# Mixture-of-experts stage: fixed blocks of 448 slots per expert with stationary weights, and the general path behind one branch at the end

## Chip, cores, metric

The kernel runs on one core of one Trainium2 chip. The metric is device time in microseconds (us), the median of several runs. The engines are called PE (matmul; PEld is its weight load), DVE, ACT, POOL and SP, as in the profile.

## The reference

A linear attention (RWKV5) over 4 batches x 8 heads x 768 steps x 48 gives 3072 tokens of 384 values. Each token goes to one of 8 experts. The expert is the argmax of 8 logits or, where a gate is open, the expert of the token before:

```python
for b in range(B):
    prev_e = -1
    for s in range(S):
        fresh_e = int(np.argmax(logits[b, s]))
        if s == 0 or local_gate[b, s] < 0.5:
            e = fresh_e
        else:
            e = prev_e if prev_e >= 0 else fresh_e
        prev_e = e
        ...                                   # p = softmax of the logits
        h = np.maximum(x[b, s] @ w1[e], 0.0)  # 384 -> 1024
        out[b, s] = p[e] * (h @ w2[e])        # 1024 -> 384
```

Everything is fp32. With the fixed input the experts get 417, 353, 336, 448, 376, 390, 329 and 423 tokens.

## The kernel before

Four stages follow one another: a chunked attention (with a branch to a general version, for decay weights outside a range); a routing on DVE that gives every token a slot; the experts; the end. Slots are cut into tiles of 128, each tile belonging to one expert. How many tiles an expert needs is only known at run time, so the loop runs over the worst case:

```python
NT = (N + E * (P - 1)) // P          # 31 tiles of 128 slots
...
with tc.If(outside > 0, label="general"):          # between attention and routing
    general_attention(...)
...
def fetch(j):                                       # weights anew for every tile
    e = nc.values_load(tex[0:1, j:j + 1], ...)      # the tile's expert, from memory
    nc.sync.dma_start(out=w1t..., in_=w1[bass.ds(e, 1)]...)
    nc.sync.dma_start(out=w2t..., in_=w2[bass.ds(e, 1)]...)
    nc.gpsimd.indirect_dma_start(out=xg, in_=x_d, in_offset=...gid[:, j:j + 1]...)
def hidden(j):                                      # w1 stationary, 128 tokens moving
    for m ...: for kk ...:
        nc.tensor.matmul(hps[:, m * P:(m + 1) * P], lhsT=w1[:, 4 * g + m, kk, :], rhs=xT[:, kk, :], ...)
def output(j):                                      # hT stationary, 384 columns of w2 moving
    for m in range(FK):
        nc.tensor.matmul(yp[:, :D], lhsT=hT[:, m, :], rhs=w2[:, m, :], ...)
    nc.vector.tensor_scalar(yo, yp[:, :D], gate[:, j:j + 1], None, Alu.mult)
    nc.gpsimd.indirect_dma_start(out=out, out_offset=...sid[:, j:j + 1]..., in_=yo, ...)
```

(`...` marks cuts.)

## Time and profile before

The median is 569.85 us (569.43 to 570.50, 4 runs). The table of windows, cut at the seams of the stages, shows where they go. Its columns are the window, its length, the busy time (and instructions) of PE, PEld, DVE, ACT and POOL, the granted TensorE clock, the DMA share and GB/s.

```profile
0.00:182.60 182.60, 158.47 (x1342) 115.31 (x1342) 134.94 (x326) 16.17 (x33) 93.06 (x61) 1.00 0.59 201
182.60:216.70 34.10, 13.18 (x56) 11.89 (x56) 17.77 (x61) 0.36 (x1) 3.87 (x14) 0.55 0.46 186
216.70:222.71 6.01, 0.87 (x3) 0.50 (x4) 0.56 (x2) 0.00 (x0) 4.03 (x4) 0.50 0.33 88
222.71:560.81 338.10, 338.10 (x2074) 272.03 (x2074) 35.28 (x60) 37.02 (x62) 56.69 (x58) 0.99 0.84 301
560.81:568.70 7.89, 0.00 (x0) 0.00 (x0) 0.62 (x1) 0.00 (x0) 0.98 (x1) 0.74 0.00 0
```

| stage | us | what sets its length |
|---|---|---|
| attention | 182.6 | untouched by the change |
| branch and routing | 34.1 | a serial chain, most of it DVE instructions; 10.5 us of it are matmuls |
| first gather and turn | 6.0 | one gather and its transposes (the turn), then the expert matmuls can begin |
| experts | 338.1 | PE: busy in every microsecond |
| end | 7.9 | scaling, one scatter, closing drain |

In the fourth row PE's busy time equals the length of the window, so the stage can only get shorter if PE gets less to do.

### The profile page before, as it was taken

The page shows a single profiled execution, that of the slowest core. Times are in us where ns is not written, and L with a number is a line of the kernel's source. Part 1 is how long each engine was busy: PE and PEld are TensorE (multiplying, and loading weights), DVE is VectorE, ACT ScalarE, POOL GpSimd, SP SyncE. Part 2 cuts the span into 40 slices and gives each one's busy share as a digit, 9 for nine tenths or more (in the row PEclk, how much of TensorE's full clock was granted, in tenths as well). Part 3 has the DMA queues.
Part 4 walks back from the last instruction along what each step waited for, and adds up shares of the span by engine and source line. Part 5 has one row for each costly group of instructions (what it writes and reads, how often), then busy time and mean ns, then how long its engine had stood idle before and what let it go on. Part 6 is the DMA issues. An engine that isn't in the chain of part 4 may idle for free. (4 is left out here: it accounts for less than half of the span.)

```text
span 568.7 us, 8584 instructions
## 1 busy us (share of the span) xinstructions
PE 510.6 (90%) x3475; PEld 399.7 (70%) x3475; DVE 189.2 (33%) x449; ACT 53.5 (9%) x96; POOL 158.6 (28%) x136
## 2 busy tenths in 40 slices
PE   0689999999998155999999999999999999999994
PEld 0567587577584155878877877887887887887782
DVE  6699679589491650111011011110110101101100
ACT  0000200200202000100110110110110011011010
POOL 6578466277211013122121121221211212110010
PEclk9999999999999555999999999999999999999998
DMA  8678847854202084688899899988899989998830
GB/s 299 225 251 283 299 165 249 278 169 155 95 29 85 2 349 164 241 319 319 320 325 338 301 341 330 327 319 335 312 330 335 321 321 311 330 311 326 306 112 0
DMA packets 28412, 145.41 MB, mean 256 GB/s; under 512 B 4336, under 2 KB 7439, under 8 KB 20432
## 3 DMA queue, kind: packets, MB, share of 16 engines
q1 hardware_dynamic: 20448, 128.98, 64.2%
q0 software_dynamic: 3968, 10.82, 5.2%
q10 hardware_dynamic: 3952, 5.00, 2.5%
q8 instruction: 29, 0.48, 0.3%
q14 instruction: 15, 0.12, 0.1%
HBM read 135.35 MB, written 10.81 MB: 257 GB/s over the span
## 5 line engine op out<-in xcount | busy, mean ns | idle before, releaser
L490 PEld LDWEIGHTS hps<-exT,w1t 128*128 128x128 f32 x1488 | 172.8, 194 | 9.0 <-DVE exT L481 1.1
L490 PE MATMUL hps<-exT,w1t 128*128 128x128 f32 x1488 | 173.1, 277 | 0.7 <-DVE exT L481 0.7
L498 PE MATMUL eyp<-w2t,hT 128*128 128x384 f32 x496 | 165.1, 486 | 0.0
L498 PEld LDWEIGHTS eyp<-w2t,hT 128*128 128x128 f32 x496 | 91.8, 190 | 57.5
L502 POOL DMA_INDIRECT out_dram<-yo,sid x31 | 31.2, 1006 | 174.9 <-DVE yo L501 174.9
L481 DVE COPY exT<-etp 128x384 f32<-128x384 f32 x31 | 17.3, 558 | 160.2 <-PE etp L479 160.2
L501 DVE TENSOR_SCALAR yo<-eyp,gate 128x384 f32<-128x384 f32 x31 | 19.2, 618 | 148.1 <-PE eyp L498 148.1
L492 ACT ACTIVATE hT<-hps 128x512 f32<-128x512 f32 x62 | 37.0, 597 | 331.2 <-PE hps L490 331.2
L471 POOL DMA_INDIRECT xg<-x_d,gid x31 | 30.5, 984 | 121.7 <-PE etp L479 107.1
L108 POOL TENSOR_TENSOR rw<-rT,pw 128x768 f32<-128x768 f32 x16 | 28.8, 1798 | 42.8 <-PE yp L159 42.0
L126 DVE SCALAR_TENSOR_TENSOR st<-st,pw,ds 64x64 f32<-64x64 f32 x128 | 35.9, 280 | 4.1
L111 POOL TENSOR_TENSOR pd<-rT,kT 128x768 f32<-128x768 f32 x16 | 29.7, 1858 | 17.1 <-PE dp L148 13.1
L110 POOL TENSOR_TENSOR ke<-k,endT 128x768 f32<-128x768 f32 x16 | 32.3, 2021 | 7.0 <-POOL rw L108 2.5
L140 DVE TENSOR_TENSOR am<-sc,mask 128x384 f32<-128x384 f32 x64 | 31.2, 550 | 0.5
L137 PE MATMUL sc<-rw,kw 64*128 64x128 f32 x384 | 27.1, 290 | 2.3 <-POOL rw L108 2.3
L165 PE MATMUL yp<-am,v 128*64 128x128 f32 x384 | 28.9, 281 | 0.0
L116 PE MATMUL ds<-v,ke 128*128 128x128 f32 x160 | 23.1, 294 | 6.3 <-POOL ke L110 6.0
L159 PEld LDWEIGHTS yp<-rw,st 128*128 128x128 f32 x160 | 20.8, 190 | 9.1 <-PE dp L148 4.2
L137 PEld LDWEIGHTS sc<-rw,kw 64*128 64x128 f32 x384 | 23.9, 196 | 4.4 <-POOL rw L108 2.6
L116 PEld LDWEIGHTS ds<-v,ke 128*128 128x128 f32 x160 | 20.2, 200 | 9.4 <-POOL ke L110 6.4
L159 PE MATMUL yp<-rw,st 128*128 128x128 f32 x160 | 25.5, 290 | 1.4 <-DVE st L126 1.4
L148 PE MATMUL dp<-pd,uz 128*128 128x384 f32 x64 | 25.5, 521 | 0.0
(128 smaller groups left out, 256.3 us busy)
## 6 DMA issues: line engine op xcount, KB each, us to landing
w1t<-in_w_dram SPq DMA_DIRECT2D x31, 1536.0 KB
w2t<-in_w_dram SPq DMA_DIRECT2D x31, 1536.0 KB
rT<-in_rT_dram SPq DMA_DIRECT2D x16, 384.0 KB
kT<-in_kT_dram SPq DMA_DIRECT2D x16, 384.0 KB
k<-in_k_dram SPq DMA_DIRECT2D x16, 384.0 KB
v<-in_v_dram SPq DMA_DIRECT2D x16, 384.0 KB
vT<-in_vT_dram SPq DMA_DIRECT2D x16, 384.0 KB
x_d<-x ACTq DMA_DIRECT2D x4, 1152.0 KB
```

The source lines that it names most:

```text
L110: nc.gpsimd.tensor_mul(ke, t["k"], spread(endT[:, hp], 1, NCH))
L111: nc.gpsimd.tensor_mul(pd, t["rT"], t["kT"])
L116: nc.tensor.matmul(ds[c // 3][:, c % 3 * P:(c % 3 + 1) * P], lhsT=ke[:, c, :], rhs=t["v"][:, c, :], start=True, stop=True)
L126: nc.vector.scalar_tensor_tensor(state[q, c, i], state[q, c - 1, i], pw[q, hp, P:P + 1], add, Alu.mult, Alu.add)
L137: nc.tensor.matmul(sc[i][:, c * P:(c + 1) * P], lhsT=kw[q, g + c, :], rhs=rw[q, g + c, :], start=True, stop=True)
L140: nc.vector.tensor_mul(am[:, i, g:g + 3], sc[i][:, :3 * P].rearrange("p (c t) -> p c t", t=P), spread(mask, 1, 3))
L159: nc.tensor.matmul(yp[:, c % 3 * P:(c % 3 + 1) * P], lhsT=t["state"][:, c - 1].rearrange("p i e -> p (i e)"), rhs=t["rw"][:, c, :], start= ...
L471: nc.gpsimd.indirect_dma_start(out=xg, out_offset=None, in_=x_d, in_offset=bass.IndirectOffsetOnAxis(ap=gid[:, j:j + 1], axis=0))
L490: nc.tensor.matmul(hps[:, m * P:(m + 1) * P], lhsT=t[j]["w1"][:, 4 * g + m, kk, :], rhs=t[j]["xT"][:, kk, :], start=(kk == 0), stop=(kk == ...
L492: nc.scalar.activation(hT[:, 4 * g:4 * g + 4].rearrange("p m t -> p (m t)"), hps, Act.Relu)
L498: nc.tensor.matmul(yp[:, :D], lhsT=t[j]["hT"][:, m, :], rhs=t[j]["w2"][:, m, :], start=(m == 0), stop=(m == FK - 1))
L502: nc.gpsimd.indirect_dma_start(out=out, out_offset=bass.IndirectOffsetOnAxis(ap=sid[:, j:j + 1], axis=0), in_=yo, in_offset=None, bounds_c ...
```

## The change

The intent is to read an expert's weights once and stream up to 448 tokens past them. Each expert gets a fixed block of 448 slots (three of 128 rows and one of 64), so no table of tiles is needed. Weights are stationary in both products. The output therefore comes out transposed, and is turned back before it is scaled and scattered. The scatters go through disjoint views of the output so that none waits for another. If an expert has more than 448 tokens, or the decay weights are out of range, one branch at the end does everything again in the general way.

```diff
-def experts(tc, wp, x_d, w1, w2, out, ident, gid, sid, gate, tex):
+def experts(tc, wp, x_d, w1, w2, out, ident, gid, sid, gate):
+    rows = [min(P, CAP - j * P) for j in range(ST)]      # 128, 128, 128, 64
+    outs = dram_disjoint_views(out, E * ST)
+        def fetch(e): ...                                # w1[e], w2[e], once per expert
+        def gather(e): ...                               # four gathers
+        def turn(e, j): ...                              # transposes in, copy to exT
+        def hidden(e, m):
+            for kk in range(DK):
+                nc.tensor.matmul(h[:, :CAP], lhsT=t[e]["w1"][:, m, kk, :], rhs=t[e]["xT"][:, kk, :], ...)
+            nc.scalar.activation(hT, h[:, :CAP], Act.Relu)
+        def output(e, m):
+            for d in range(DK):
+                nc.tensor.matmul(t[e]["y"][d][:, :CAP], lhsT=t[e]["w2"][:, m, d * P:(d + 1) * P],
+                                 rhs=t[e][m], start=(m == 0), stop=(m == FK - 1))
+        def drain(e): ...                                # y from PSUM: one ACT copy, two DVE copies
+        def send(e, j): ...                              # transposes back, gate, scatter to outs[c]
...
-    with tc.If(outside > 0, label="general"):
-        general_attention(tc, rT, kT, v, wu, wg_d, x_d, ident, lt)
...
+    experts(tc, wp, x_d, w1, w2, out, ident, gid, sid, gate)
+    some = nc.values_load(rare[0:1, 1:2], ...)
+    with tc.If(some > 0, label="rare"):
+        ...                                              # general attention if needed, routing, 31 tiles
```

The routing loses the instructions for the table of tiles and gains three for the slot and two for the overflow count.

More of the change, by code (lines that the diff above doesn't have):

```diff
@@ L6 @@
 from concourse._compat import with_exitstack
+from concourse.bass_types import dram_disjoint_views
 from concourse.masks import make_identity
@@ L31 @@
 NT = (N + E * (P - 1)) // P
+ST = 4
+CAP = 448
 FRESH_TO = -1.5 * 2.0 ** -23
@@ L286, in general_attention, with route @@
             nc.vector.tensor_copy(lt[:, c, :], lp[:, :E + 1])
-def route(tc, once, ps, lt, mask, ident, gid, sid, gate, tex):
+def route(tc, once, ps, lt, mask, ident, gid, sid, gate, tex=None, over=None):
     nc = tc.nc
+    nt = NT if tex is not None else E * ST
     def tl(name, shape, dt=F32):
@@ L312, in route @@
     iq = iota("iq", [P, P], [[1, P]])
-    ij = iota("ij", [P, NT], [[1, NT]])
+    ij = iota("ij", [P, nt], [[1, nt]])
     t8 = iota("t8", [P, NC], [[E * P, NC]], base=1, cm=E)
@@ L391, in route @@
     nc.vector.tensor_tensor(cnt, bound[:, 1:], bound[:, :E], op=Alu.subtract)
-    ti = tl("ti", [P, E], I32)
-    nc.vector.tensor_scalar(ti, cnt, float(P - 1), None, Alu.add)
-    nc.vector.tensor_scalar(ti, ti, 7, None, Alu.arith_shift_right)
-    tf = tl("tf", [P, E])
-    nc.vector.tensor_copy(tf, ti)
-    stop = tl("stop", [P, E])
-    nc.vector.tensor_tensor_scan(stop, ones[:, :E], tf, 0.0, Alu.mult, Alu.add)
-    le = tl("le", [P, NT, E])
-    nc.vector.tensor_tensor(le, spread(stop, 1, NT), spread(ij, 2, E), op=Alu.is_le)
-    tj = tl("tj", [P, NT])
-    nc.vector.tensor_reduce(tj, le, axis=AX.X, op=Alu.add)
-    nc.vector.tensor_scalar(tex, tj[0:1], float(E - 1), None, Alu.min)
-    sh = tl("sh", [P, E])
-    nc.vector.tensor_tensor(sh, stop, tf, op=Alu.subtract)
-    nc.vector.scalar_tensor_tensor(sh, sh, float(P), bound[:, :E], Alu.mult, Alu.subtract)
+    sh = tl("sh", [P, E])
+    if tex is None:
+        nc.vector.tensor_scalar(sh, bound[:, :E], -1.0, None, Alu.mult)
+        big = tl("big", [1, E])
+        nc.vector.tensor_scalar(big, cnt[0:1], float(CAP), None, Alu.is_gt)
+        nc.vector.tensor_reduce(over, big, axis=AX.X, op=Alu.add)
+    else:
+        ti = tl("ti", [P, E], I32)
+        nc.vector.tensor_scalar(ti, cnt, float(P - 1), None, Alu.add)
+        nc.vector.tensor_scalar(ti, ti, 7, None, Alu.arith_shift_right)
+        tf = tl("tf", [P, E])
+        nc.vector.tensor_copy(tf, ti)
+        stop = tl("stop", [P, E])
+        nc.vector.tensor_tensor_scan(stop, ones[:, :E], tf, 0.0, Alu.mult, Alu.add)
+        le = tl("le", [P, NT, E])
+        nc.vector.tensor_tensor(le, spread(stop, 1, NT), spread(ij, 2, E), op=Alu.is_le)
+        tj = tl("tj", [P, NT])
+        nc.vector.tensor_reduce(tj, le, axis=AX.X, op=Alu.add)
+        nc.vector.tensor_scalar(tex, tj[0:1], float(E - 1), None, Alu.min)
+        nc.vector.tensor_tensor(sh, stop, tf, op=Alu.subtract)
+        nc.vector.scalar_tensor_tensor(sh, sh, float(P), bound[:, :E], Alu.mult, Alu.subtract)
     nc.vector.tensor_tensor(pos, pos, spread(sh, 2, NC), op=Alu.add)
@@ L412, in route @@
     nc.vector.tensor_reduce(slot, pos.rearrange("p e c -> p c e"), axis=AX.X, op=Alu.add)
+    if tex is None:
+        far = tl("far", [P, NC])
+        nc.vector.tensor_scalar(far, slot, float(CAP), float(4 * E * ST * P), Alu.is_ge, Alu.mult)
+        nc.vector.tensor_tensor(slot, slot, far, op=Alu.add)
+        nc.vector.scalar_tensor_tensor(slot, ef, float(ST * P), slot, Alu.mult, Alu.add)
     si = tl("si", [P, 2, NC], I32)
@@ L428, in route @@
     nc.vector.tensor_tensor(pe, pe, sm, op=Alu.mult)
-    val = tl("val", [P, NC, 2, NT])
-    nc.vector.tensor_tensor(val[:, :, 0, :], spread(sf[:, 1], 2, NT), spread(ij, 1, NC), op=Alu.is_equal)
-    nc.gpsimd.tensor_tensor(val[:, :, 1, :], val[:, :, 0, :], spread(pe, 2, NT), op=Alu.mult)
-    nc.vector.tensor_tensor(val[:, :, 0, :], val[:, :, 0, :], spread(t1, 2, NT), op=Alu.mult)
+    val = tl("val", [P, NC, 2, nt])
+    nc.vector.tensor_tensor(val[:, :, 0, :], spread(sf[:, 1], 2, nt), spread(ij, 1, NC), op=Alu.is_equal)
+    nc.gpsimd.tensor_tensor(val[:, :, 1, :], val[:, :, 0, :], spread(pe, 2, nt), op=Alu.mult)
+    nc.vector.tensor_tensor(val[:, :, 0, :], val[:, :, 0, :], spread(t1, 2, nt), op=Alu.mult)
     ohq = tl("ohq", [P, NC, P])
@@ L441, in route @@
         for c in range(g, g + G):
-            nc.tensor.matmul(mp[:, :2 * NT], lhsT=ohq[:, c, :],
+            nc.tensor.matmul(mp[:, :2 * nt], lhsT=ohq[:, c, :],
                              rhs=val[:, c].rearrange("p a j -> p (a j)"),
                              start=(c == 0), stop=(c == NC - 1))
-    tok = tl("tok", [P, NT])
-    nc.vector.tensor_copy(tok, mp[:, :NT])
-    nc.vector.tensor_copy(gate, mp[:, NT:2 * NT])
+    tok = tl("tok", [P, nt])
+    nc.vector.tensor_copy(tok, mp[:, :nt])
@@ L448, in route, with fetch, gather, turn @@
+    nc.vector.tensor_copy(gate, mp[:, nt:2 * nt])
     nc.vector.tensor_scalar(gid, tok, -1.0, 0.0, Alu.add, Alu.max)
-    none = tl("none", [P, NT])
+    none = tl("none", [P, nt])
     nc.vector.tensor_scalar(none, tok, 0.0, float(4 * N), Alu.is_equal, Alu.mult)
     nc.vector.scalar_tensor_tensor(sid, tok, -1.0, none, Alu.add, Alu.add)
-def experts(tc, wp, x_d, w1, w2, out, ident, gid, sid, gate, tex):
+def experts(tc, wp, x_d, w1, w2, out, ident, gid, sid, gate):
+    nc = tc.nc
+    rows = [min(P, CAP - j * P) for j in range(ST)]
+    outs = dram_disjoint_views(out, E * ST)
+    with tc.tile_pool(name="xp", bufs=2) as xp, tc.tile_pool(name="gp", bufs=6) as gp, \
+         tc.tile_pool(name="hp", bufs=3) as hp, tc.tile_pool(name="yp", bufs=2) as yp, \
+         tc.tile_pool(name="op", bufs=4) as op, \
+         tc.tile_pool(name="yps", bufs=1, space=PSUM) as yps, \
+         tc.tile_pool(name="hps", bufs=3, space=PSUM) as hps, \
+         tc.tile_pool(name="tps", bufs=2, space=PSUM) as tps:
+        t = [dict() for _ in range(E)]
+        def fetch(e):
+            w1t = wp.tile([P, FK, DK, P], F32, name="w1t")
+            nc.sync.dma_start(out=w1t.rearrange("p m k f -> p (m k f)"), in_=w1[e])
+            w2t = wp.tile([P, FK, D], F32, name="w2t")
+            nc.sync.dma_start(out=w2t.rearrange("p m f -> p (m f)"), in_=w2[e])
+            t[e].update(w1=w1t, w2=w2t)
+        def gather(e):
+            t[e]["xg"] = []
+            for j, n in enumerate(rows):
+                xg = gp.tile([P, D], F32, name="xg")
+                nc.gpsimd.indirect_dma_start(
+                    out=xg[:n], out_offset=None, in_=x_d,
+                    in_offset=bass.IndirectOffsetOnAxis(ap=gid[:n, e * ST + j:e * ST + j + 1], axis=0),
+                    bounds_check=N - 1, oob_is_err=False)
+                t[e]["xg"].append(xg)
+        def turn(e, j):
+            n = rows[j]
+            if j == 0:
+                t[e]["xT"] = xp.tile([P, DK, CAP], F32, name="exT")
+            tp = tps.tile([P, DK, P], F32, name="etp", tag="tp")
+            for kk in range(DK):
+                nc.tensor.transpose(tp[:, kk, :n], t[e]["xg"][j][:n, kk * P:(kk + 1) * P], ident[:n, :n])
+            nc.vector.tensor_copy(t[e]["xT"][:, :, j * P:j * P + n], tp[:, :, :n])
+        def hidden(e, m):
+            h = hps.tile([P, 512], F32, name="h")
+            for kk in range(DK):
+                nc.tensor.matmul(h[:, :CAP], lhsT=t[e]["w1"][:, m, kk, :], rhs=t[e]["xT"][:, kk, :],
+                                 start=(kk == 0), stop=(kk == DK - 1))
+            hT = hp.tile([P, CAP], F32, name="hT")
+            nc.scalar.activation(hT, h[:, :CAP], Act.Relu)
+            t[e][m] = hT
+        def output(e, m):
+            if m == 0:
+                t[e]["y"] = [yps.tile([P, 512], F32, name=f"y{d}") for d in range(DK)]
+            for d in range(DK):
+                nc.tensor.matmul(t[e]["y"][d][:, :CAP], lhsT=t[e]["w2"][:, m, d * P:(d + 1) * P],
+                                 rhs=t[e][m], start=(m == 0), stop=(m == FK - 1))
+        def drain(e):
+            t[e]["yT"] = yT = yp.tile([P, DK, CAP], F32, name="yT")
+            for d in range(DK):
+                (nc.scalar.copy if d == 0 else nc.vector.tensor_copy)(yT[:, d], t[e]["y"][d][:, :CAP])
+        def send(e, j):
+            n, c = rows[j], e * ST + j
+            tp = tps.tile([P, DK, P], F32, name="otp", tag="tp")
+            for d in range(DK):
+                nc.tensor.transpose(tp[:n, d], t[e]["yT"][:, d, j * P:j * P + n], ident)
+            yo = op.tile([P, D], F32, name="yo")
+            nc.vector.tensor_scalar(yo[:n], tp[:n].rearrange("p d x -> p (d x)"), gate[:n, c:c + 1], None,
+                                    Alu.mult)
+            nc.gpsimd.indirect_dma_start(
+                out=outs[c], out_offset=bass.IndirectOffsetOnAxis(ap=sid[:n, c:c + 1], axis=0),
+                in_=yo[:n], in_offset=None, bounds_check=N - 1, oob_is_err=False)
+        fetch(0)
+        fetch(1)
+        gather(0)
+        for j in range(ST):
+            turn(0, j)
+        for e in range(E):
+            if 1 <= e and e + 1 < E:
+                fetch(e + 1)
+            if e + 1 < E:
+                gather(e + 1)
+            for m in range(FK):
+                hidden(e, m)
+                if e and 1 <= m <= ST:
+                    send(e - 1, m - 1)
+                if m:
+                    output(e, m - 1)
+                if e + 1 < E and FK - ST <= m:
+                    turn(e + 1, m - (FK - ST))
+            output(e, FK - 1)
+            drain(e)
+        for j in range(ST):
+            send(E - 1, j)
@@ L456, in experts, with general_experts @@
+def general_experts(tc, wp, x_d, w1, w2, out, ident, gid, sid, gate, tex):
     nc = tc.nc
@@ L566 @@
     chunked_attention(tc, rT, kT, vT, k, v, x_d, w_t[:, :, 0], uz_d, wp_d, mask, ident, lt)
-    outside = nc.values_load(flag[0:1, 0:1], min_val=0, max_val=P * HP,
-                             skip_runtime_bounds_check_because="a count of entries")
-    with tc.If(outside > 0, label="general"):
-        general_attention(tc, rT, kT, v, wu, wg_d, x_d, ident, lt)
-    gid = keep.tile([P, NT], I32, name="gid")
-    sid = keep.tile([P, NT], I32, name="sid")
-    gate = keep.tile([P, NT], F32, name="gate")
@@ L576 @@
-    tex = keep.tile([1, NT], I32, name="tex")
+    gid = keep.tile([P, E * ST], I32, name="gid")
+    sid = keep.tile([P, E * ST], I32, name="sid")
+    gate = keep.tile([P, E * ST], F32, name="gate")
+    over = keep.tile([1, 2], F32, name="over")
+    rare = keep.tile([1, 2], I32, name="rare")
     wp = ctx.enter_context(tc.tile_pool(name="wp", bufs=2))
     with tc.tile_pool(name="ro", bufs=1) as ro, tc.tile_pool(name="rps", bufs=8, space=PSUM) as rps:
-        route(tc, ro, rps, lt, mask, ident, gid, sid, gate, tex)
@@ L581 @@
-    experts(tc, wp, x_d, w1, w2, out, ident, gid, sid, gate, tex)
+        route(tc, ro, rps, lt, mask, ident, gid, sid, gate, over=over[:, 0:1])
+        nc.vector.tensor_copy(over[:, 1:2], flag)
+        nc.vector.tensor_copy(rare[:, 0:1], flag)
+        nc.vector.tensor_tensor(rare[:, 1:2], over[:, 0:1], over[:, 1:2], op=Alu.add)
+    experts(tc, wp, x_d, w1, w2, out, ident, gid, sid, gate)
+    why = "a count of entries"
+    some = nc.values_load(rare[0:1, 1:2], min_val=0, max_val=P * HP + E, skip_runtime_bounds_check_because=why)
@@ new lines @@
+    with tc.If(some > 0, label="rare"):
+        outside = nc.values_load(rare[0:1, 0:1], min_val=0, max_val=P * HP, skip_runtime_bounds_check_because=why)
+        with tc.If(outside > 0, label="general"):
+            general_attention(tc, rT, kT, v, wu, wg_d, x_d, ident, lt)
+        with tc.tile_pool(name="rk", bufs=1) as rk:
+            g_gid = rk.tile([P, NT], I32, name="g_gid")
+            g_sid = rk.tile([P, NT], I32, name="g_sid")
+            g_gate = rk.tile([P, NT], F32, name="g_gate")
+            g_tex = rk.tile([1, NT], I32, name="g_tex")
+            with tc.tile_pool(name="gro", bufs=1) as ro, tc.tile_pool(name="grps", bufs=8, space=PSUM) as rps:
+                route(tc, ro, rps, lt, mask, ident, g_gid, g_sid, g_gate, tex=g_tex)
+            general_experts(tc, wp, x_d, w1, w2, out, ident, g_gid, g_sid, g_gate, g_tex)
```

## The prediction

> **What bounds the kernel now.** I read the page first: the lane view and the groups of instructions. Then I read the table of windows, to split the span into stages, then the timeline of one expert tile, then the timeline and the branch records at the two seams (end of the attention, end of the kernel).
>
> ```profile
> L490 PE MATMUL hps<-exT,w1t 128*128 128x128 f32 x1488 | 173.1, 277 | 0.7 <-DVE exT L481 0.7
> L498 PE MATMUL eyp<-w2t,hT 128*128 128x384 f32 x496 | 165.1, 486 | 0.0
> ```
>
> The expert stage works through 31 tiles of 128 slots. A tile has 24 products for the hidden layer and 8 for the output, but the groups count 48 and 16: each fp32 product is two instructions. The busy sums only locate the work; 277 and 486 ns are latencies of overlapping instructions. The last column says that the matmuls wait for nothing.
>
> ```profile
> 300.00:400.00 100.00, 100.00 (x622) 80.66 (x621) 11.20 (x19) 10.75 (x18) 18.58 (x19) 1.00 0.91 325
> ```
>
> This row of the windows table (PE, PEld, DVE, ACT, POOL, then clock, DMA share, GB/s) shows 100 us of the expert stage: PE is busy for all of it at full clock. DMA is at 0.91, so it looks like a second bound, but no PE wait points to it.
>
> ```profile
> 300.63 5.52 PE L490 MATMUL hps<-exT,w1t 128*128 128x128 f32 x48
> 305.99 0.49 PE L479 MATMUL etp<-ident,xg 128*128 128x128 f32 x3
> 306.31 5.33 PE L498 MATMUL eyp<-w2t,hT 128*128 128x384 f32 x16
> ...
> 311.48 5.52 PE L490 MATMUL hps<-exT,w1t 128*128 128x128 f32 x48
> ```
>
> One tile in the timeline. Start to start gives what a stream costs: hidden (305.99-300.63)/48 = 111.7 ns per instruction of 128 moving columns; transposes (306.31-305.99)/3 = 107 ns; output (311.48-306.31)/16 = 323 ns per 384 columns. One tile is 10.85 us; 31 are 336.4 us, 59% of the span.
>
> **What the Trainium skill says.** (1) "TensorE: Matmul & The Clock Gate", section "Back-to-back issue gap", gives N/2.4 + 2.5 ns per warm matmul of N columns, and "LDWEIGHTS" makes a load depend on its columns alone. The trace agrees in form but not in rate: (323-111.7)/256 = 0.826 ns a column, about twice 1/2.4, for each of the two instructions of an fp32 product. Widening the moving side thus buys only the small constant (111.7 - 128 x 0.826 = 6 ns), since weight loads already overlap. (2) The same page's Part 1 says that the array starts at half clock until it has been busy for some microseconds. The trace agrees: granted clock 0.50 in the routing, and the first tile's 48 hidden instructions take 7.51 us from 222.71 instead of 5.36. (3) "Runtime: NRT & Kernel Launch", section "Instruction fetch mechanics", says that a taken branch out of the prefetched pages stalls for a fetch. The trace agrees:
>
> ```profile
> L570 PEldq COMPARE_BRANCH  x1: 3512/3512/3512, 182.6 to 182.6; - x1
> ```
>
> This is the jump over the general attention (branch records of that line, ns). (4) "DMA: Bandwidth & Descriptors", section "SWDGE vs HWDGE vs iDMA", says that a GpSimd core computes the descriptors of indirect DMAs in software. The trace agrees: every gather or scatter holds POOL about 1 us, and consecutive gathers start 1.26 us apart (219.25, 220.51, 221.76).
>
> **The change, part by part.**
>
> *Expert matmuls.* Per expert 24 hidden and 24 output products, two instructions each: 96 instructions of 448 columns. By the trace's two points one costs 111.7 + 320 x 0.826 = 376 ns, so 36.1 us. Transposes: 12 in (their moving side is the identity, 9 of 128 and 3 of 64 columns) and now also 12 out, since the output comes out transposed: 24 at about 109 ns = 2.6 us. An expert is 38.7 us, eight 309.6. The first expert's inward 12 and the last's outward 12 lie outside the stretch from first hidden to last output matmul: 309.6 - 2.6 = 307.0, plus the same 2.15 us for the cold start (7.51-5.36) = 309.1. Before, that stretch runs from 222.71 to 560.81 = 338.1. **Gain 29.0 us.** Check by columns: slots fall from 31 x 128 = 3968 to 8 x 448 = 3584, 9.7% of 336 = 32.5 us; the new transposes return 96 x 0.107 = 10.3; the removed per-instruction constants (31 x 64 instructions become 8 x 96) yield 1216 x 6 ns = 7.3. Net 29.5.
>
> *Weights.* 31 fetches of 3 MB become 8, an estimated 10 us of DMA (3.1 MB at the 325 GB/s shown) in each 38.7 us. They were hidden, so this takes nothing off the path; DMA in the expert stage should fall from 0.9 to about 0.25-0.3.
>
> *The branch moves.* Before, this seam costs DVE 4.1 us:
>
> ```profile
> 182.37 0.21 DVE L192 COPY lt<-lq 128x54 f32<-128x54 f32 x1 [8.37 <-PE lq L190]
> ...
> 186.69 0.35 DVE L321 TENSOR_REDUCE mx<-lt 128x24 f32<-128x192 f32 x1 [3.79 <-DVEq L570]
> ```
>
> The logits are ready at 182.58 and their use starts at 186.69. Without the branch, it can start at about 182.7: **-4.0 us**, since routing is one serial chain on DVE from there.
>
> *Routing.* Off the chain go the tile-to-expert table's instructions: from cnt (197.03) to the add of sh (199.04) 2.0 us becomes about 0.8 (cnt, sh, big, over at 0.2). Three small ones for the slot are added (0.6). **-0.6 us.** The 48 matmuls L442 (10.3 us at half clock, bound by their weight loads) go from 62 to 64 columns: no change.
>
> *First gather.* Before, the first hidden matmul needs one gather; now it needs four of one expert. Starts are 1.5 then 1.26 us apart, so the fourth starts 4.0 us after the first; it has half the rows. **+3.8 us.** Later gathers run a whole expert ahead.
>
> *Expert boundary.* Accumulators are single-buffered: y is drained by one ACT copy and two DVE copies (estimated 0.65 us each from 0.56 for 384 columns), 1.3 us after the last matmul. PE meanwhile has 12 hidden instructions of the next expert, 4.5 us, before it needs the drained data. The same slack covers ReLU (0.60 us) and the turn copies. **0.**
>
> *The end.*
>
> ```profile
> 555.48 5.33 PE L498 MATMUL eyp<-w2t,hT 128*128 128x384 f32 x16
> 555.68 0.60 ACT L492 ACTIVATE hT<-hps 128x512 f32<-128x512 f32 x1 [2.02 <-PE hps L490]
> 560.84 0.62 DVE L501 TENSOR_SCALAR yo<-eyp,gate 128x384 f32<-128x384 f32 x1 [9.90 <-PE eyp L498]
> 561.74 0.98 POOL L502 DMA_INDIRECT out_dram<-yo,sid  x1 [9.54 <-DVE yo L501]
> ```
>
> Before: last matmul ends 560.81, span ends 568.7: 7.9 us, of which 6.95 follow the start of the scatter. After: the third accumulator's copy (+0.7; the other two overlap the last matmuls), three transposes (+0.6), the scaling and the step to POOL (0.9): the first scatter starts at about +2.3. Three more at 1.26 (the disjoint views let them follow without waiting for each other's landing): +6.1. Then 6.95 as before: +13.1. To this comes the jump over the rare path. Each engine meets it after its own last work, so only POOL's (and whatever waits for all) is exposed: between nothing and the 3.5 us of PE's jump plus a 0.5 us load of the flag; I take 3. Total 16.1: **+8.2 us.**
>
> Sum: -29.0 - 4.0 - 0.6 + 3.8 + 8.2 = -21.6, so 570.2 - 21.6 = 548.6.
>
> **Does the rare path run?** I computed the routing on the host from the reference: the experts get 417, 353, 336, 448, 376, 390, 329 and 423 tokens. The largest fills 448 exactly and the test is "greater than", so it is skipped. It is a knife edge: one differently routed token would run everything twice.
>
> **Rivals.** (a) *DMA was the true bound* (0.91 busy, SP waits for PE to free weight buffers). Then removing 3/4 of the weight traffic would release more than the column count says, and the time could go to 530. Against it: zero idle before L490 and L498, and a tile that is the sum of its streams. (b) *Boundary stalls*: if the transposes back, interleaved between accumulating matmuls, or the single accumulator set made PE wait 1-2 us per expert, 8-16 us would return: 557-564. For it: y has one buffer. Against it: the 4.5 us of slack worked out above. (c) *The end grows more*: the four scatters are ordered after all, one landing (about 2 us) each, and the jump costs all its 4 us on top of POOL's closing drain: 555-557. (d) *The removed branch yields nothing*, because engines still wait at the attention's end for buffers: 552.
>
> **Range and chances.** The matmul term is firm to 2 us (rate read from the same engine, type and tiles). Head and tail are each good to some 4 us; the errors together give 542 to 556. Faster by over 2% means below 558.8; that fails only with (b) or several misses: 0.92 faster, 0.07 same, 0.01 slower.
>
> **What would show it.** Hidden and output matmuls 384 instructions each, starts 376 ns apart; PE busy 100% at clock 1.00 between experts; DMA share there below 0.3; mx starting near 182.7 and the first hidden matmul near 222; last matmul near 531; 14-18 us from it to the end, with POOL scatters 1.26 us apart. I would be wrong if starts at 448 columns are not on the line through 128 and 384, if PE idles at each expert's second block, or if the tail passes 20 us.

## The result, and the profile after

The changed kernel takes 550.31 us (550.23 to 551.93, 4 runs) against 569.85 us. The ratio is 0.9663, with a 95% interval of 0.9642 to 0.9684. Ratios here are the mean time of one kernel's fast runs over that of the other's in the same rounds, so they are not quite the ratio of the medians quoted.

The same table of windows for the changed kernel, cut at its own seams:

```profile
0.00:182.40 182.40, 158.18 (x1342) 114.98 (x1342) 134.72 (x328) 16.20 (x33) 93.26 (x61) 1.00 0.60 202
182.40:211.65 29.25, 13.19 (x56) 11.89 (x56) 16.89 (x60) 0.36 (x1) 4.12 (x14) 0.55 0.51 212
211.65:221.79 10.14, 3.65 (x14) 2.38 (x15) 2.03 (x4) 0.00 (x0) 7.27 (x7) 0.50 0.37 100
221.79:532.35 310.56, 310.56 (x936) 161.36 (x935) 40.83 (x71) 39.10 (x72) 52.60 (x53) 0.99 0.25 89
532.35:548.50 16.15, 2.06 (x13) 1.07 (x11) 2.90 (x5) 0.00 (x0) 3.86 (x4) 0.63 0.14 45
```

Subtracting row by row: the experts gain 27.5 us, branch and routing 4.9, the attention 0.2 (noise). The head gives back 4.1 and the end 8.3. The sum is -20.2, the difference of the spans (568.7 and 548.5). The DMA share of the expert stage has fallen from 0.84 to 0.25, and PE is still busy throughout.

The expert matmuls, in the page's groups:

```profile
L518 PE MATMUL h<-exT,w1t 128*128 128x448 f32 x384 | 155.6, 545 | 0.0
L528 PE MATMUL y<-hT,w2t 128*128 128x448 f32 x384 | 155.4, 541 | 0.0
```

There are 768 instructions in place of 1984, each of 448 columns, and they wait for nothing (last column). Their timeline across the start of an expert shows the pace:

```profile
300.22 4.67 PE L518 MATMUL h<-exT,w1t 128*128 128x448 f32 x12
304.73 0.49 PE L540 MATMUL otp<-ident,yT 128*128 128x128 f32 x3
305.06 2.42 PE L528 MATMUL y<-hT,w2t 128*128 128x448 f32 x6
307.32 2.42 PE L518 MATMUL h<-exT,w1t 128*128 128x448 f32 x6
```

(304.73-300.22)/12 = 376 ns, (305.06-304.73)/3 = 110 ns for a transpose back. The outputs at 305.06 follow without a gap although the single set of accumulators had to be drained first. The drain's last DVE copy ended at 301.05, well before its data was needed.

The seam where the branch was, on DVE:

```profile
182.20 0.21 DVE L196 COPY lt<-lq 128x54 f32<-128x54 f32 x1 [8.37 <-PE lq L194]
...
182.66 0.35 DVE L328 TENSOR_REDUCE mx<-lt 128x24 f32<-128x192 f32 x1
```

The logits are ready at 182.42 and used from 182.66: the 4.1 us of before are 0.24. The head, on PE:

```profile
218.78 1.49 PE L512 MATMUL etp<-ident,xg 128*128 128x128 f32 x6 [0.58 <-DMA xg<-x_d,gid]
221.34 0.66 PE L512 MATMUL etp<-ident,xg 128*128 128x128 f32 x2 [1.07 <-DMA xg<-x_d,gid]
221.79 0.95 PE L518 MATMUL h<-exT,w1t 128*128 128x448 f32 x1
```

Expert 0 needs four gathers, of which PE turns the last two in the first line. The two transposes at 221.34 belong to *expert 1*. The scheduler has put them ahead of the first hidden matmul, and they wait 1.07 us for a gather that nothing urgent needs.

The end, first POOL's timeline, then single records of the branch's line and of the closing line (count, shortest/median/longest in ns, first and last start):

```profile
534.33 0.98 POOL L544 DMA_INDIRECT out_dram<-yo,sid  x1 [18.17 <-DVE yo L542]
...
538.19 0.92 POOL L544 DMA_INDIRECT out_dram<-yo,sid  x1 [0.30 <-issue]
```

```profile
L704 PEldq COMPARE_BRANCH  x1: 4197/4197/4197, 535.2 to 535.2; - x1
L704 POOLq INC_SWDGE_SEM  x1: 1468/1468/1468, 540.9 to 540.9; - x1
L765 POOLq DRAIN  x3: 40/107/5300, 542.4 to 548.2; - x3
```

The last scatter is issued by 539.11. PE's jump over the rare path is long, 4.2 us, but over at 539.4. POOL then waits at the branch's end for the landings of the scatters (its semaphores at 539.5 to 540.8; the last landing is at 540.78), does a step of 1.47 us at 540.89, and only at 542.39 begins the drain of 5.3 us that ends the kernel: 8.6 us from the last issue to the drain's end. In the kernel before POOL goes into this drain at once:

```profile
L631 POOLq DRAIN  x3: 45/113/6348, 561.5 to 568.4; - x3
```

It started at 561.50, overlapped the scatter (issued by 562.72), and ended at 567.85: 5.1 us.

### The profile page after: what moved, and what is told of

It is laid out like the page before. It is cut to its first block, busy times and chain, and to the rows that moved or that the text cites. A ratio compares the mean times of both kernels' runs of the same rounds, so it can differ in the third digit from the quotient of the medians.

```text
span 548.5 us, 6145 instructions
## 1 busy us (share of the span) xinstructions
PE 487.6 (89%) x2358; PEld 291.7 (53%) x2358; DVE 197.4 (36%) x467; ACT 55.7 (10%) x106; POOL 161.1 (29%) x138
## 4 chain that ended last, share of the span: by engine, by line
issue 52%; DVE 18%; PE 15%; POOL 12%; DMA 1%; POOLq 1%; ACT 0%
POOL out_dram L544 6%; DVE st L130 5%; POOL xg L500 5%; PE lp L189 4%; DVE kw L113 4%; DVE am L144 4%; PE mp L461 2%; PE tp L180 2%; PE yp L169 2%; DVE xT L172 2%; DVE own L154 2%; PE yp L163 2%; PE ds L120 1%; PE sc L141 1%; DVE st L128 1%
## 5 line engine op out<-in xcount | busy, mean ns | idle before, releaser
L518 PE MATMUL h<-exT,w1t 128*128 128x448 f32 x384 | 155.6, 545 | 0.0
L528 PE MATMUL y<-hT,w2t 128*128 128x448 f32 x384 | 155.4, 541 | 0.0
L518 PEld LDWEIGHTS h<-exT,w1t 128*128 128x128 f32 x384 | 72.2, 193 | 64.7 <-issue 64.7
L528 PEld LDWEIGHTS y<-hT,w2t 128*128 128x128 f32 x384 | 70.2, 190 | 58.8 <-issue 58.3
L513 DVE COPY exT<-etp 128x384 f32<-128x384 f32 (+1 forms) x32 | 16.2, 508 | 132.6 <-PE etp L512 131.7
L521 ACT ACTIVATE hT<-h 128x448 f32<-128x448 f32 x64 | 34.8, 544 | 285.4 <-PE h L518 242.9
L542 DVE TENSOR_SCALAR yo<-otp,gate 128x384 f32<-128x384 f32 (+1 forms) x32 | 19.5, 615 | 118.7 <-PE otp L540 118.6
L500 POOL DMA_INDIRECT xg<-x_d,gid x32 | 32.4, 1013 | 101.4 <-PE etp L512 85.4
L181 ACT COPY x<-tp 128x384 f32<-128x384 f32 x24 | 11.2, 480 | 141.8 <-PE tp L180 141.6
```

Of the source, the lines that this page charges most:

```text
L500: nc.gpsimd.indirect_dma_start(out=xg[:n], out_offset=None, in_=x_d, in_offset=bass.IndirectOffsetOnAxis(ap=gid[:n, e * ST + j:e * ST + j ...
L518: nc.tensor.matmul(h[:, :CAP], lhsT=t[e]["w1"][:, m, kk, :], rhs=t[e]["xT"][:, kk, :], start=(kk == 0), stop=(kk == DK - 1))
L521: nc.scalar.activation(hT, h[:, :CAP], Act.Relu)
L528: nc.tensor.matmul(t[e]["y"][d][:, :CAP], lhsT=t[e]["w2"][:, m, d * P:(d + 1) * P], rhs=t[e][m], start=(m == 0), stop=(m == FK - 1))
```

## The experiments

Every kernel below was correct. Where a kernel is right on this input only, its expectation says so.

**1. The changed kernel without its branch (a_nobranch).**

```diff
-    some = nc.values_load(rare[0:1, 1:2], ...)
-    with tc.If(some > 0, label="rare"):
-        ...
```

> The changed kernel without the rare path at its end (same result on this input). Theory: in the trace of the changed kernel the last scatter's issue ends at 539.11 and POOL's closing drain at 547.69, 8.6 us later; in the kernel before 562.72 and 567.85, 5.1 us. The 3.4 us between them are POOL waiting for the landings and its own semaphore step (1.47 us) before the drain can begin, so without the branch the time falls by 3.4 us, to about 546.9, and drain and last scatter lie 5.1 us apart again. Rival, as the prediction put it: what is exposed is PE's jump (4.2 us, over at 539.43); that is past before POOL's landings are, so on this view nothing changes, 550.3. Second rival: the drain lasts 5.3 us from wherever it starts and is not tied to the last scatter; then the end moves by the removed steps alone, 2 to 3 us.

Measured: 546.64 us (545.64 to 547.67, 5 runs), ratio 0.9597. The closing records:

```profile
L750 POOLq DRAIN  x3: 45/102/8450, 534.9 to 544.1; - x3
```

The drain now begins at 534.86, beside the scatters, and ends at 543.31. That is 5.3 us after the last scatter's issue (538.01) instead of 8.6: 3.3 us, as the theory had it. This run takes away PE's jump together with POOL's steps, so it can't tell the two apart alone. Experiment 10 can: there PE's jump is over at 524.10, before the last scatter is issued (526.33), and the drain still ends 8.6 us after that issue (534.89). PE's jump is not what the end waits for. The second rival is half right: the data fit a drain of 5.3 us that counts from its start or from the last scatter's issue, whichever is later.

**2. The kernel before without its branch (b_nobranch).**

```diff
-    outside = nc.values_load(flag[0:1, 0:1], ...)
-    with tc.If(outside > 0, label="general"):
-        general_attention(tc, rT, kT, v, wu, wg_d, x_d, ident, lt)
```

> The kernel before without the branch over the general attention (same result on this input). Theory: the first use of the logits moves from 4.1 us after they are ready to about 0.2 us, and everything after it is one chain: 569.85 - 3.9 = 566.0. Rival: engines wait at this seam for buffers of the attention anyway, and nothing or less than 1 us comes off: 569 to 570.

Measured: 565.19 us (564.77 to 566.67, 6 runs), ratio 0.9930 (0.9911 to 0.9949). In the trace the step from the logits to their use is 0.25 us (181.64 to 181.89) instead of 4.1. The theory holds. So the branch costs about 4 us in the middle and 3.3 us at the end: moving it gained under 1 us.

**3. Ordered scatters (a_oneview).**

```diff
-    outs = dram_disjoint_views(out, E * ST)
+    outs = [out] * (E * ST)
```

> The changed kernel with all 32 scatters through one view of the output, so that they are ordered. Theory: between experts they are 4.8 us apart and a landing takes about 2.1 us, so nothing changes there; in the last burst of four each must wait for the landing of the one before, so the step grows from 1.28 us to about 2.4 us, 3 x 1.1 = +3.4 us: about 553.7. Rival: the waits stand in POOL's queue ahead of gathers, gathers come late, PE waits for the turned tokens and every expert loses 1 us or more: over 558.

Measured: 557.34 us (556.85 to 558.04, 5 runs), ratio 0.9782. The stretch from first hidden to last output matmul is 310.8 us, as without the ordering, so the rival is out. The last burst on POOL:

```profile
534.89 0.98 POOL L544 DMA_INDIRECT out_dram<-yo,sid  x1 [18.17 <-DVE yo L542]
538.40 0.98 POOL L544 DMA_INDIRECT out_dram<-yo,sid  x1 [2.53 <-DMA out_dram<-yo,sid]
542.26 0.98 POOL L544 DMA_INDIRECT out_dram<-yo,sid  x1 [2.88 <-DMA out_dram<-yo,sid]
```

Each scatter waits for the landing of the one before. The place was right and the size too small: the steps are 3.5 and 3.9 us, and 3.3 us to the fourth scatter (at 545.60), not 2.4. A landing takes 2.6 to 3.1 us from the start of the issue for these three, and 0.77 us pass from it to the start of the next. The views are worth about 7 us, all of it at the end.

**4. The old weight traffic put back (a_traffic).**

```diff
...                                # a pool jp of two buffers for the extra reads
+        def again(e, m):
+            for src in (w1, w2):
+                junk = jp.tile([P, FK * D], F32, name="junk")
+                nc.sync.dma_start(out=junk, in_=src[e])
...
+                if m % 3 == 1:
+                    again(e, m)
```

> The changed kernel with the weights of each expert read three more times into buffers that nobody reads, which brings the DMA share of the expert stage from 0.25-0.33 back to about 0.9 as in the kernel before. Theory: PE bounds the expert stage and weight traffic was hidden, so the stretch from first hidden to last output matmul stays at 310.6 us within 1 us; the first gather may land up to 2 us later beside the extra reads: 550 to 553. Rival (DMA was the true bound, the saved traffic is where the gain comes from): most of the 19.5 us come back, over 565.

Measured: 558.63 us (557.05 to 558.91, 4 runs), ratio 0.9808. Two rows of its windows table, one inside the stage and one over nearly all of it:

```profile
300.00:400.00 100.00, 100.00 (x309) 52.23 (x308) 15.25 (x27) 13.00 (x24) 19.92 (x20) 1.00 0.92 350
229.00:539.00 310.00, 310.00 (x935) 161.14 (x934) 40.83 (x71) 39.02 (x72) 49.47 (x50) 0.99 0.76 296
```

Inside the stage DMA is as busy as before the change (0.92 against 0.91; over the whole stage 0.76 against 0.84), and PE still never waits: the stretch is 310.2 us. The 8 us that the kernel lost are mostly at the head, where my allowance of 2 us was too small. The extra reads run ahead of the work, beside the first gathers, and the first hidden matmul starts at 228.7 instead of 221.8. Weight traffic costs nothing in the stage, but a burst of it delays a gather that PE waits for: over the run the median time from issue to landing is 6.6 us for a gather and 7.2 us for a scatter, against 3.1 and 2.5 us in the changed kernel (`--dma`).

**5. Fewer slots, nothing else (b_nt28).**

```diff
-NT = (N + E * (P - 1)) // P
+NT = 28
```

> The kernel before with its tile count cut from the worst case of 31 to the 28 that this input needs (417, 353, 336, 448, 376, 390, 329, 423 tokens are 4, 3, 3, 4, 3, 4, 3, 4 tiles); right on this input only. It has then 28 x 128 = 3584 slots, as many as the 8 x 448 of the change, but none of its weight reuse, wide moving side or transposes back. Theory: the gain of the change is the smaller number of slots; three tiles of 10.85 us fall away: 569.9 - 32.6 = 537.3, faster than the changed kernel. Rival: holding the weights and streaming 448 columns is what gains; then 28 small tiles with 86 MB of weight reads stay above the changed kernel's 550.3.

Measured: 537.55 us (536.79 to 537.79, 4 runs), ratio 0.9425. The old loop over as many slots as the change has, 3584, beats the changed kernel by 13 us. Its stretch is 305.7 us, against 310.6 for the wide blocks. The theory holds.

**6. Weight reuse without the wide blocks (a_tiles128).**

```diff
-CAP = 448
+CAP = 512
...
+            e = j // ST
+            if j % ST == 0:          # w1t, w2t read once per expert, used by its four tiles of 128
+                ...
```

(The rest of `experts` is the kernel before's tile loop.)

> The changed kernel with fixed blocks of 4 x 128 slots per expert, worked through in tiles of 128 as the kernel before does (no transposes back, one scatter at the end, one gather before the first hidden matmul), but with the weights read once per expert. It tells weight reuse from slot count. Theory: 32 tiles x 10.85 + 2.15 = 349.4 us of stretch against 310.6 (+38.8), one gather instead of four at the head (-4.1), 11.6 us from last matmul to the end instead of 16.2 (-4.6): 550.3 + 30.1 = 580.4. The DMA share in the stage should be about 0.3. Rival (reading weights once per expert is what gains): 32 tiles run faster than 10.85 us each, and the time is under 565.

Measured: 580.45 us (580.24 to 580.53, 4 runs), ratio 1.0181. The stretch is 349.3 us. A row of its windows table:

```profile
300.00:400.00 100.00, 100.00 (x619) 80.39 (x619) 11.14 (x19) 11.34 (x19) 18.83 (x19) 1.00 0.35 125
```

DMA falls to 0.35 and the tiles run no faster. Reading the weights once per expert is worth nothing by itself.

**7. Wider blocks (a_cap512).**

```diff
-CAP = 448
+CAP = 512
```

> The changed kernel with 512 slots per expert instead of 448 (same result). Theory: time follows the columns at 0.826 ns each: an instruction takes 111.7 + 384 x 0.826 = 429 ns instead of 376, 768 of them make +40.9; the block of 64 rows and its 0.2 us per expert go away (-1.5): 550.3 + 39.4 = 589.7. Rival: at 448 columns something other than the columns sets the pace (weight loads, drains, boundaries), and 64 more columns cost under 20 us: below 570.

Measured: 591.64 us (588.79 to 592.58, 4 runs), ratio 1.0360. Its PE timeline:

```profile
322.14 2.74 PE L528 MATMUL y<-hT,w2t 128*128 128x512 f32 x6
324.72 2.74 PE L518 MATMUL h<-exT,w1t 128*128 128x512 f32 x6
```

(324.72-322.14)/6 = 430 ns, and the stretch grows by 39.8 us to 350.4: the columns set the pace up to 512. The rest of the excess is at the end, 17.8 us here. With 4096 slots the wide blocks need 350.4 us and the tiles of experiment 6 need 349.3: at the same number of slots the wide blocks are not faster here either.

**8. The next expert's transposes kept back (a_order).**

```diff
-                    turn(e + 1, m - (FK - ST))
...                                # t[e]["last"] is the last hidden matmul so far
+                    with tc.issue_after(t[e]["last"]):
+                        turn(e + 1, m - (FK - ST))
```

> The changed kernel with the transposes of the next expert kept behind the hidden matmuls that the program puts before them. In the trace of the changed kernel two of the three transposes of expert 1's first block (221.34) run before the first hidden matmul (221.79) and wait for a gather, while all of expert 0's tokens had been turned by 220.67. Theory: the first hidden matmul starts at about 220.7, 1.1 us earlier, and nothing else moves: 549.2. Rival: the half clock of the first microseconds lasts until about 226.1 whatever PE does, so an earlier start only runs more at half speed and gains half of it or less: 549.8 to 550.3.

Measured: 548.99 us (548.52 to 550.61, 5 runs), ratio 0.9635 (0.9619 to 0.9651). This interval overlaps the changed kernel's, so the times alone do not decide. In the trace the first hidden matmul starts 9.0 us after the slots are ready (210.67 to 219.71) instead of 10.1, so the wait of 1.1 us is gone. The stretch is 0.4 us longer, since the two transposes are now inside it and more of it runs at half clock. Net about 0.7 us by these two profiles, between the two theories.

**9. Whole rows in the last block (a_pad).**

```diff
-            for j, n in enumerate(rows):
+            for j, n in enumerate([P] * ST):
...
-                nc.tensor.transpose(tp[:, kk, :n], t[e]["xg"][j][:n, kk * P:(kk + 1) * P], ident[:n, :n])
+                nc.tensor.transpose(tp[:, kk, :], t[e]["xg"][j][:, kk * P:(kk + 1) * P], ident)
```

> The changed kernel with 128 instead of 64 rows gathered and turned for each expert's last block (the extra 64 columns are not copied out). In the trace of the changed kernel the three transposes with 64 rows start 0.09 us late, and the matmul after the first following one starts 0.10 us late, because their weight loads aren't run ahead: 0.42 + 0.10 us against 0.33. Theory: 0.2 us x 7 experts = -1.4 us, though three transposes of 128 columns replace three of 64: 548.9. Rival: the gaps are of the profile's modelled starts only, or the longer transposes eat the gain: 550.3 within 0.4.

Measured: 548.31 us (547.45 to 549.24, 5 runs), ratio 0.9612. The changed kernel's PE timeline at such a block:

```profile
295.57 2.04 PE L528 MATMUL y<-hT,w2t 128*128 128x448 f32 x5
297.54 0.40 PE L512 MATMUL etp<-ident,xg 64*128 64x64 f32 x3
297.87 2.52 PE L528 MATMUL y<-hT,w2t 128*128 128x448 f32 x6
300.22 3.17 PE L518 MATMUL h<-exT,w1t 128*128 128x448 f32 x8
```

and the padded one's:

```profile
296.55 0.49 PE L512 MATMUL etp<-ident,xg 128*128 128x128 f32 x3
296.88 2.42 PE L528 MATMUL y<-hT,w2t 128*128 128x448 f32 x6
299.14 4.30 PE L518 MATMUL h<-exT,w1t 128*128 128x448 f32 x11
```

After 64 rows the next six outputs take 2.35 us (297.87 to 300.22), after 128 rows 2.26 (296.88 to 299.14). The wait of 0.09 us in front of the transposes (five outputs of 376 ns from 295.57 end at 297.45, the transposes start at 297.54) is gone too. The stretch falls by 1.7 us to 308.8: doing twice the work is faster here. The rival is out. The padding changes the rows and the moving columns of these transposes together (64 to 128 each), so which of the two causes the delay after them was not separated.

**10. A version that beats both (best_tiles).** The kernel before's tile loop with 28 tiles and the changed kernel's branch at the end:

```diff
+USUAL = 28
...
+    if over is not None:
+        nc.vector.tensor_scalar(over, stop[0:1, E - 1:E], float(USUAL), None, Alu.is_gt)
...
-    with tc.If(outside > 0, label="general"):
-        general_attention(...)
...
+    experts(tc, wp, x_d, w1, w2, out, ident, gid, sid, gate, tex, USUAL)
+    with tc.If(some > 0, label="rare"):
+        ...                            # as in the change; routing and experts with 31 tiles
```

> A version meant to beat both and right for every input: the tile loop of the kernel before with 28 tiles, and the changed kernel's rare path at the end, taken when the experts need more than 28 tiles or the weights of the decay lie outside (it then does everything again with 31 tiles). From the kernel before: three tiles -32.6, branch gone from the middle -4.7 (measured), branch at the end +3.7 (measured): 569.9 - 33.6 = 536.3. Rival: the tail of the branch costs more here because general and usual scatters share one view and the jump is longer: up to 540.

Measured: 536.65 us (535.99 to 537.45, 4 runs), ratio 0.9409. It is 6% faster than the kernel before and, by the ratio of the ratios, 2.6% faster than the changed one. Its last three stages:

```profile
212.70:218.59 5.89, 0.87 (x3) 0.50 (x4) 0.56 (x1) 0.00 (x0) 3.99 (x4) 0.50 0.33 92
218.59:524.42 305.83, 305.83 (x1873) 246.13 (x1873) 31.74 (x54) 33.43 (x56) 50.75 (x52) 0.99 0.83 300
524.42:535.70 11.28, 0.00 (x0) 0.00 (x0) 0.62 (x1) 0.00 (x0) 0.98 (x1) 0.61 0.03 10
```

It keeps the short head (5.9 us against 10.1) and one scatter at the end (11.3 against 16.2), and its expert stage is 4.7 us shorter.

**11 and 12. One slot too few (a_cap447), one tile too few (best_27).** These run the rare paths.

```diff
-CAP = 448                -USUAL = 28
+CAP = 447                +USUAL = 27
```

> The changed kernel with 447 slots per expert, one too few for the fourth expert's 448 tokens, so that the rare path runs. It should be correct, and shows what the path costs: after about 540 us come the load of the flag and the jump (some 5 us), the routing (34 us from logits to slots), the first gather and turn (6 us), 31 tiles (338 us) and the end (8 us): about 930 us. If it takes much less, the general path isn't what runs; if it is wrong, the path is broken.

> The version with 28 tiles, cut to 27, one too few, so that its own rare path runs and is shown to be correct. One tile less than its 536.7, then the same repetition of routing and 31 tiles, some 390 us: about 915 us.

Measured, one run each: 920.15 us and 898.59 us, both correct. My sums were 10 and 16 us too high. In the first run the second routing starts at 539.67 (I had about 545), its first hidden matmul follows after 35.5 us (I had 40), and the end after the last matmul is 4.7 us (I had 8). The overflow part of both rare paths works; the general attention inside them was not run. Both designs sit on an edge with this input: expert 3 fills its 448 slots exactly, and the input needs exactly 28 tiles.

## Why the prediction was right

The predicted 548.6 us is within 2 us of the measured 550.31. The steps, against the two traces:

| step | predicted | traces |
|---|---|---|
| expert matmuls | -29.0 | -27.5 |
| branch out of the middle | -4.0 | -3.9 |
| routing | -0.6 | -1.0 |
| first gather | +3.8 | +4.1 |
| the end | +8.2 | +8.3 |

*Expert matmuls.* The line through 128 and 384 columns held at 448 (376 ns) and at 512 (430 ns). The formula of the Trainium skill that the prediction set beside it is, by its page, the gap of an isolated matmul (see the last section); the sum did not use it. The missing 1.5 us are the blocks of 64 rows, which cost more than the 109 ns per transpose that I gave them; padding them gains 1.7 us in the stage.

*Slots, not reuse.* My check by columns said where the gain comes from, and experiments 5 and 6 confirm it. Slots alone, in the old loop, make the stage 32.4 us shorter (338.1 to 305.7). Weight reuse alone makes no tile faster. The wide blocks add the transposes back and lose their gain from fewer instructions again: 310.6 against 305.7 us for the same number of slots. The change is faster because it computes 3584 slots instead of 3968, not because its weights stand still.

*Branch and routing.* The branch's 3.9 us came off as stated. The routing gained 0.4 us more because the add of `sh` did not have to wait for the overflow count, which the scheduler put behind it (0.27 us from `cnt` to the add, where I had 0.8).

*First gather.* The size was right by two errors that cancel. Four gathers delay the first matmul by about 3.0 us rather than 3.8 (experiment 8: 9.0 against 6.0 us), and 1.1 us come from expert 1's transposes ahead of the first hidden matmul, which I did not foresee.

*Boundaries.* The predicted cost of zero held: no wait in front of any hidden or output matmul.

*The end.* The size was right, a part of the mechanism wrong. I wrote that the exposed part lies between nothing and "the 3.5 us of PE's jump plus a 0.5 us load of the flag". PE's jump took 4.2 us and was hidden (experiment 10). What shows is POOL waiting at the branch's end for the last scatter's landing (1.7 us from 539.11) and then its 1.47 us step before the drain may start, 3.3 us in all (experiment 1). That the 3 us I took for the jump nearly equals this is luck.

*The rivals.* (a) is out by experiments 4 and 6. (b) by the traces. (c) is what happens without the views: 557.34 us in experiment 3, near the 555 to 557 that I had given for ordered scatters and a fully exposed jump, though all of it came from the scatters. (d) is out by experiment 2.

What stays open: the closing drain ended 1.5 to 1.9 us after the last scatter's issue in the two runs through the rare path, against 4.6 to 5.3 us in the kernels without a branch at the end, and no run says why. In all other runs the drain's length goes with the number of indirect DMAs (gathers and scatters) before it: 4.65 us after 56 (experiments 5 and 10), 5.14 after 62 (the kernel before) and 5.30 after 64 (the changed kernel), 83 ns each. This is a pattern over the traces that no experiment was made to test, and the two rare-path runs, with 126 and 116, break it. The attention's end also moved between 181.4 and 183.1 us from one profile to the next with the same attention code; differences under 1 us should be read from a stage, not from the span.

## What to carry to other kernels

When one engine is busy throughout, count what it is given to do before changing how it does it: here three padded tiles cost more than the whole restructuring gained, and one constant, with a fallback behind it, removed them. A transfer engine that is 90% busy is not a bound until something is seen to wait for it; putting the traffic back is a cheap test. Bursts at the head and the end of a stage (four gathers before the first matmul, four scatters after the last, a branch in front of the closing drain) have little or nothing to hide behind, so take them into the sum.

## What the Trainium skill lacked or had wrong

- "TensorE: Matmul & The Clock Gate", section "Back-to-back issue gap", has no figure for fp32. Its N/2.4 + 2.5 ns is, by the page, the gap of an isolated matmul. Four times that, an estimate of 223, 650, 757 and 863 ns at 128, 384, 448 and 512 columns, fits what an fp32 product took here with its two instructions in a stream: 223, 646, 752 and 860 ns. The factor of four stands on another page: "FP8 and Floating Point Precision", section "TensorE Precision Notes", gives true fp32 four passes.
- The same TensorE page, Part 3, "The mechanism", says that weight loads overlap running matmuls only where the row groups differ. The trace differs: loads of all 128 rows ran beside matmuls of all 128 rows throughout (both start every 376 ns, and a load is done while the matmul that started with it still runs). The section's mention of a background weight buffer fits this better. Loads of 64 rows between such matmuls came late; padding rows and columns to 128 gained 1.7 us in eight experts.
- "DMA: Bandwidth & Descriptors", section "Anatomy of one DMA — SWDGE (gpsimd) path", gives about 2.0 us fixed per DMA plus bytes / 436e3, an estimate of 2.45 us for a scatter of 128 x 384 fp32 values. The trace agrees where DMA has little else to do (median 2.5 us in the changed kernel) and differs beside the weight reads of the old loop: 8.7 us in b_nt28 at a DMA share of 0.91. The section has no figure for ordered scatters, here 3.3 to 3.9 us from one to the next.
- No page gives a time for a closing drain on POOL like the one here: it ends 4.6 to 5.3 us after the last scatter's issue in kernels without a branch at the end, and 8.5 to 10.1 us with one that is skipped.
- "Runtime: NRT & Kernel Launch", section "Instruction fetch mechanics", gives no figure for the stall of a taken branch: on PE the recorded jumps took 3.5 us in the kernel before and 4.2 us in the changed one, on ACT, POOL and DVE 45 to 72 ns.
